# A gating kernel with larger tiles in fewer slots: 60 rows in four instead of 44 in six

## The chip, the cores and the metric

The kernel runs on one core of one Trainium2 chip. The metric is the device time of one execution in microseconds (us); the time before is the median of 9 runs.

## The reference

The input x has the shape 1x384x384x384 in bf16, the weight w1d is one number. Every channel is averaged over all 147,456 positions, the average is multiplied by the weight and put through a sigmoid, and every position of x is multiplied by the 384 numbers that result.

```python
g = jnp.einsum("bhwc->bc", x) / (H * W)
s = sigmoid(g * w1d[0])          # k = 1: one tap, no padding
return x * s[:, None, None, :]
```

So x has to be read (113.25 MB) and an output of the same size has to be written.

## The kernel before, in words

The 147,456 positions are 1152 "rows" of 128 positions: a row is a 128x384 tile in bf16, 768 bytes in each of 128 partitions. A tile of n rows is laid out so that every partition holds n x 768 bytes that are contiguous in memory on both sides (`dram`, line 172). All tiles live in one buffer, the arena.

The kernel gambles. It computes an early gate, `s_early`, from the first 4 rows alone, multiplies every tile by it and stores it, so that x is read once. Meanwhile TensorE adds up all rows, which gives the full gate, `s_true`. In the end VectorE compares the two gates bit for bit after rounding to bf16 (lines 399 to 418), and SP, ACT and VectorE read the flag `redo`. Only when it is set do they run the second pass (`again`, lines 422 to 446), which reads x again and multiplies by the full gate.

Five numbers set the tiling (line 158): the first tile has FIRST = 8 rows, the early gate is made of EARLY = 4 of them, the other 1144 rows are 26 tiles of TILE = 44 rows, which go round SLOTS = 6 places of the arena, and the first BOTH = 4 of these are loaded in two halves, one on SP's queue and one on ACT's. The first tile has its place behind the slots, at row `base` = 264.

The order of the work is written out by hand through a small planner, which keeps a stream of instructions per engine and inserts the waits that reads and writes of rows ask for:

- SP issues all other loads, in order (`load`, line 221). The load of tile k into its slot waits for the store of tile k - 6 (lines 378 to 381).
- TensorE multiplies each tile by a matrix of ones, in matmuls of 128x512 (`add_rows`, line 250), adding into three PSUM banks. It runs a loop over the slots (line 288); GpSimd waits for a tile's loads and then raises the semaphore `ready` (`relay`, line 119), on which TensorE waits at line 279.
- VectorE multiplies the tile by the early gate in place (`gate`, lines 199 to 202), after TensorE has read it, since the product overwrites the tile.
- ACT issues the store (`put`, line 316), in order, on its own DMA queue.

ACT's queue also carries the load of the weight, `w_one`, behind the first half tile (line 360); TensorE spreads the weight over the partitions (line 337) before it sums the first rows, and the early gate waits for both (line 367). After the last tile come the store of the first tile (line 387), the addition of the banks (line 390), the full gate (line 391) and the comparison. The full gate is written to the first row of the slot that the next tile would have had, `slot(26)` (line 218); the second pass first copies it to row `base` (lines 424 to 430), because its own tiles use the slots.

Of the kernel before, what the change touches and what calls it, by code (L numbers as in the profile page):

```python
# [149 lines left out]
def split(n, most):  # L150
    k = -(-n // most)
    return [n // k + (i < n % k) for i in range(k)]
# [2 lines left out]
WIDE = 512  # L155


FIRST, EARLY, TILE, SLOTS, BOTH = 8, 4, 44, 6, 4


def bass_standalone__channel_attn_eca__vision_kernel(
# [7 lines left out]
    n_rows = B * H * W // P  # L169
    x_rows, o_rows = x.flatten_outer_dims(), out.flatten_outer_dims()  # L170

    def dram(view, r0, n):
        return view[r0 * P : (r0 + n) * P, :].rearrange("(p t) c -> p (t c)", p=P)
# [10 lines left out]
    n_arena = nc.sbuf_bytes_remaining // (2 * C)  # L184
# [7 lines left out]
    def at(r0, n):  # L192
        assert r0 + n <= n_arena
        return arena[:, r0 * C : (r0 + n) * C]

    def rows(r0, n):
        return [("sb", r) for r in range(r0, r0 + n)]

    def gate(to, place, n, s):
        s_b = s[:].unsqueeze(1).broadcast_to([P, n, C])  # L200
        v, to_v = (at(r, n).rearrange("p (t c) -> p t c", t=n) for r in (place, to))
        return lambda e: e.tensor_tensor(to_v, v, s_b, ALU.mult)  # L202

    n_tiles = (n_rows - FIRST) // TILE
    base = SLOTS * TILE
    assert (n_rows - FIRST) % TILE == 0 and base + FIRST <= n_arena
    assert FIRST % 4 == EARLY % 4 == TILE % 4 == 0 and EARLY < FIRST
    last = n_tiles - 1
    ready = nc.alloc_semaphore("ready")
# [1 line left out]
    def slot(k):  # L211
        return k % SLOTS * TILE
# [2 lines left out]
        return FIRST + k * TILE  # L215


    s_true = at(slot(n_tiles), 1)
    plan = Planner(nc, "a", 70)

    def load(place, n, r0, queues=("sync",)):
# [139 lines left out]
    for k in range(BOTH, SLOTS):  # L361
# [10 lines left out]
        reads=["total", "w_scaled0", "warm1"],  # L372
        writes=["s_early"],
# [11 lines left out]
    for k in range(n_tiles - SLOTS, n_tiles):  # L385
# [8 lines left out]
            s_true, total[:], ACT_F.Sigmoid, scale=w_scaled[:, 1:2]  # L394
        ),
        reads=["total", "w_scaled1"],
        writes=["s_true"] + rows(slot(n_tiles), 1),
    )
    plan.op(
        "vector",  # L400
# [3 lines left out]
        reads=["s_true", "s_early"],  # L404
        writes=["total"],
# [4 lines left out]
        reads=["total"],  # L410
        writes=["wrong"],
# [4 lines left out]
        reads=["wrong"],  # L416
        writes=["redo"],
# [3 lines left out]

    again = Planner(nc, "b", 30)
    half, r0 = base // 2, 0
    s_kept = at(base, 1)
    again.op(
        "vector",
        lambda e: e.tensor_copy(s_kept, s_true),
        reads=rows(slot(n_tiles), 1),
        writes=["s_kept"],
    )  # L430
    for k, n in enumerate(split(n_rows, half)):
        place = k % 2 * half
        again.dma("sync", at(place, n), dram(x_rows, r0, n), writes=rows(place, n))
        again.op(
            "vector",
            gate(place, place, n, s_kept),
            reads=["s_kept"] + rows(place, n),
            writes=rows(place, n),
        )
        again.final.append(  # L440
            again.dma("scalar", dram(o_rows, r0, n), at(place, n), reads=rows(place, n))
        )
        r0 += n
# [93 lines left out]
```

## Time and profile before

| what | before |
|---|---|
| median of 9 runs | 529.23 us (528.99 to 529.73) |
| the profiled execution, its own time | 529.08 us |
| its span, first to last instruction | 527.5 us |
| TensorE busy | 246.6 us (47%) |
| VectorE busy | 241.1 us (46%) |
| DMA, bytes moved and mean rate over the span | 226.53 MB, 429 GB/s |
| one gate of 44 rows on VectorE | 8.96 us |
| store of 44 rows, median from issue to landing | 52.9 us |
| load of 44 rows, median from issue to landing | 48.0 us |
| mean granted TensorE clock | 0.740 |

How to read it: the page gives shares of busy time over the whole span, and a table by stage gives for each stretch of time its length, the busy time and number of instructions of TensorE, its weight loads, VectorE, ACT and GpSimd, then the granted TensorE clock, the mean busy share of the 16 DMA engines and the GB/s that they moved. "SPq" and "ACTq" are the DMA queues of SP and ACT, "PEq" is TensorE's sequencer. The time from issue to landing of a DMA includes its waiting behind others on its queue. Times of single packets and of landings in the text are from the trace's DMA records.

### The profile page before, as it was taken

How to read it: one execution, taken by the hardware profiler on the slowest of the kernel's cores; microseconds unless marked ns; L12 is line 12 of the kernel's file. 1: busy time of each engine (PE TensorE's matmuls, PEld its weight loads, DVE VectorE, ACT ScalarE, POOL GpSimd, SP SyncE). 2: the span in 40 equal slices, each digit the busy share in tenths (PEclk: the TensorE clock that was granted, in tenths of full speed). 3: DMA queues.
4: the chain of work that ended last, by engine and by line, in shares of the span. 5: the costliest groups of instructions: out<-in, count | busy, mean ns of one | idle time of the engine just before them, and what ended most of it. 6: DMA issues, size and time to landing. Idle time of an engine off the chain costs nothing. (4 is left out here: it accounts for less than half of the span.)

```text
span 527.5 us, 1110 instructions
## 1 busy us (share of the span) xinstructions
PE 246.6 (47%) x868; PEld 0.2 (0%) x2; DVE 241.1 (46%) x45; ACT 2.7 (1%) x4; POOL 0.3 (0%) x6
## 2 busy tenths in 40 slices
PE   0876562662551652752641642743742633734700
PEld 0000000000000000000000000000000000000000
DVE  0198626336426336236336246246156246155190
ACT  1000000000000000000000000000000000000000
POOL 0000000000000000000000000000000000000000
PEclk9997866756867867757867868757767868768765
DMA  9999999999999999999999999999999999999998
GB/s 382 432 429 410 441 425 443 418 446 425 436 438 428 443 418 446 423 438 436 430 438 423 443 425 438 436 430 438 423 443 420 441 436 428 443 420 446 416 443 358
DMA packets 8357, 226.53 MB, mean 429 GB/s; under 512 B 930, under 2 KB 930, under 8 KB 1186
## 3 DMA queue, kind: packets, MB, share of 16 engines
q10 hardware_dynamic: 4466, 121.90, 53.6%
q1 hardware_dynamic: 3888, 104.60, 46.2%
q8 instruction: 1, 0.02, 0.0%
q14 instruction: 2, 0.02, 0.0%
HBM read 113.25 MB, written 113.25 MB: 429 GB/s over the span
## 5 line engine op out<-in xcount | busy, mean ns | idle before, releaser
L238 PE MATMUL acc<-arena,ones 128*128 128x512 bf16 x863 | 245.4, 455 | 241.7 <-PEq L279 241.7
L202 DVE TENSOR_TENSOR arena<-arena,s_early 128x16896 bf16<-128x16896 bf16 (+1 forms) x27 | 234.5, 8691 | 259.5 <-PE acc L238 259.5
L337 PE MATMUL w_all<-w_one,ones 1*128 1x1 bf16 x1 | 0.2, 158 | 12.7 <-DMA w_one<-in_w1d_dram 12.7
L346 DVE TENSOR_SCALAR w_scaled<-w_all 128x1 f32<-128x1 f32 x2 | 0.2, 153 | 11.7 <-PE w_all L337 11.7
L311 DVE TENSOR_TENSOR total<-total,acc 128x128 f32<-128x128 f32 (+2 forms) x11 | 4.5, 407 | 0.3
L393 ACT ACTIVATE arena<-total,w_scaled 128x384 bf16<-128x384 f32 x1 | 0.6, 614 | 496.0 <-DVE total L311 496.0
L331 ACT ACT_TABLE_LOAD x1 | 1.3, 1283 | 2.9 <-issue 2.9
L309 DVE COPY total<-acc 128x384 f32<-128x384 f32 x1 | 0.6, 558 | 1.2 <-PE acc L238 1.2
L401 DVE TENSOR_TENSOR total<-arena,s_early 128x384 f32<-128x384 uint16 x1 | 0.6, 557 | 0.7 <-ACT arena L393 0.7
L238 PE MATMUL acc<-zeros,ones 128*128 128x512 bf16 x3 | 0.8, 379 | 0.0
L369 ACT ACTIVATE s_early<-total,w_scaled 128x384 bf16<-128x384 f32 x1 | 0.6, 616 | 12.6 <-DVE total L311 12.6
L355 DVE MEMSET ones<- 128x128 bf16 x1 | 0.2, 165 | 1.0 <-PEq L522 1.0
L236 PE MATMUL acc<-arena,ones 128*128 128x512 bf16 x1 | 0.6, 607 | 0.0
L409 DVE TENSOR_REDUCE wrong<-total 128x1 f32<-128x384 f32 x1 | 0.6, 552 | 0.0
L331 ACT ACTIVATE warm<-warm 128x1 f32<-128x1 f32 x1 | 0.2, 203 | 0.0
L415 DVE CAST redo<-wrong 128x1 int32<-128x1 f32 x1 | 0.2, 153 | 0.0
L337 PEld LDWEIGHTS w_all<-w_one,ones 1*128 1x128 bf16 x1 | 0.1, 100 | 12.7 <-issue 12.7
L236 PEld LDWEIGHTS acc<-arena,ones 128*128 128x128 bf16 x1 | 0.1, 103 | 0.0
L522 POOL MEMSET const-uint8-127<- 128x1 uint8 x1 | 0.1, 102 | 0.0
L522 POOL MEMSET const-bfloat16-1.0<- 128x1 bf16 x1 | 0.1, 101 | 0.0
L354 POOL MEMSET zeros<- 128x2 bf16 x1 | 0.1, 100 | 0.0
L353 POOL MEMSET warm<- 128x1 f32 x1 | 0.1, 99 | 0.5 <-POOLq L522 0.5
(2 smaller groups left out, 0.2 us busy)
## 6 DMA issues: line engine op xcount, KB each, us to landing
out_dram<-arena ACTq DMA_DIRECT2D x26, 4224.0 KB, 52.9
arena<-in_x_dram SPq DMA_DIRECT2D x22, 4224.0 KB, 48.0
arena<-in_x_dram ACTq DMA_DIRECT2D x4, 2112.0 KB, 26.1
arena<-in_x_dram SPq DMA_DIRECT2D x4, 2112.0 KB, 30.5
arena<-in_x_dram SPq DMA_DIRECT2D x1, 768.0 KB, 7.0
out_dram<-arena ACTq DMA_DIRECT2D x1, 768.0 KB, 16.4
w_one<-in_w1d_dram ACTq DMA_DIRECT2D x1, 0.0 KB
```

The costliest lines, as they stand in the source:

```text
L202: return lambda e: e.tensor_tensor(to_v, v, s_b, ALU.mult)
L236: loaded.append(e.matmul(bank, weights, moving, start=start, stop=stop))
L238: return e.add_instruction(mybir.InstMatmult(name=nc.get_next_instruction_name(), engine=mybir.EngineType.PE, ins=[e.lower_ap(moving), e.l ...
L309: emit = lambda e, part=part, of=of: e.tensor_copy(part, of)
L311: emit = lambda e, part=part, of=of: e.tensor_tensor(part, part, of, ALU.add)
L331: lambda e: e.activation(warm[:, 1:2], warm[:, 0:1], ACT_F.Sigmoid),
L337: lambda e: e.matmul(w_all[:, 0:1], ones[0:1, :], w_one[0:1, 0:1], start=True, stop=True),
L346: lambda e, i=i, n=n: e.tensor_scalar_mul(w_scaled[:, i : i + 1], w_all[:, 0:1], 1.0 / float(P * n)),
L369: lambda e: e.activation(s_early[:], total[:], ACT_F.Sigmoid, scale=w_scaled[:, 0:1]),
L393: lambda e: e.activation(s_true, total[:], ACT_F.Sigmoid, scale=w_scaled[:, 1:2]),
L401: lambda e: e.tensor_tensor(total[:], s_true.bitcast(U16), s_early[:].bitcast(U16), ALU.not_equal),
L409: lambda e: e.reduce_max(wrong[:], total[:], axis=mybir.AxisListType.X),
```

## The change

The five numbers become FIRST = 12, EARLY = 4, TILE = 60, SLOTS = 4 and BOTH = 3. The first tile has 12 rows, of which the early gate still uses 4; the other 1140 rows are 19 tiles of 60 rows, which go round four places; the first three are loaded in halves of 30 rows on both queues, the fourth whole on SP's. In the arena 252 rows hold tiles, where it was 272. The full gate gets a row of its own behind the first tile, so its activation no longer counts as a write to a slot, and the second pass uses it there without a copy.

```diff
-FIRST, EARLY, TILE, SLOTS, BOTH = 8, 4, 44, 6, 4
+FIRST, EARLY, TILE, SLOTS, BOTH = 12, 4, 60, 4, 3
...
-    assert (n_rows - FIRST) % TILE == 0 and base + FIRST <= n_arena
+    assert (n_rows - FIRST) % TILE == 0 and base + FIRST < n_arena
...
-    s_true = at(slot(n_tiles), 1)
+    s_true = at(base + FIRST, 1)
...
-        writes=["s_true"] + rows(slot(n_tiles), 1),
+        writes=["s_true"],
...
-    s_kept = at(base, 1)
-    again.op(
-        "vector",
-        lambda e: e.tensor_copy(s_kept, s_true),
-        reads=rows(slot(n_tiles), 1),
-        writes=["s_kept"],
-    )
...
-            gate(place, place, n, s_kept),
-            reads=["s_kept"] + rows(place, n),
+            gate(place, place, n, s_true),
+            reads=rows(place, n),
```

## The prediction

> **What bounds the kernel now.** I read the page first: the engine shares, the 40 slices, the DMA totals.
>
> ```profile
> DMA  9999999999999999999999999999999999999998
> GB/s 382 432 429 410 441 425 443 418 446 425 436 438 428 443 418 446 423 438 436 430 438 423 443 425 438 436 430 438 423 443 420 441 436 428 443 420 446 416 443 358
> DMA packets 8357, 226.53 MB, mean 429 GB/s; under 512 B 930, under 2 KB 930, under 8 KB 1186
> HBM read 113.25 MB, written 113.25 MB: 429 GB/s over the span
> ```
>
> The DMA engines are busy in every slice, while TensorE and VectorE are under half busy. The bytes are those of reading x once and writing the output once, and no tile size changes them. So I cut the span at the landing of the first store (62.66), of store 20 (461.94), of the last load (490.36) and at the issue of the last large store (509.36), and asked for a table by stage.
>
> ```profile
> 0.00:62.66 62.66, 37.77 (x139) 0.20 (x2) 31.95 (x13) 2.10 (x3) 0.33 (x6) 0.92 1.00 417
> 62.66:461.94 399.28, 188.74 (x660) 0.00 (x0) 178.99 (x21) 0.00 (x0) 0.00 (x0) 0.72 1.00 433
> 461.94:490.36 28.42, 9.60 (x33) 0.00 (x0) 15.83 (x2) 0.00 (x0) 0.00 (x0) 0.73 1.01 436
> 490.36:509.36 19.00, 10.47 (x36) 0.00 (x0) 8.99 (x2) 0.00 (x0) 0.00 (x0) 0.77 0.99 428
> 509.36:527.50 18.14, 0.00 (x0) 0.00 (x0) 5.33 (x10) 0.61 (x1) 0.00 (x0) 0.50 0.89 380
> ```
>
> The last column is GB/s. The middle is flat at 433; only the head (417) and the last 18 us (380) are below. At 433.4 the 226.53 MB take 522.7 us, so 4.8 of the 527.5 us are all that is not plain transfer: 1.05 us to the first packet, about 1.1 us more in the head (10-us windows there show 369 and 409 GB/s), and the rest in the last microseconds, where the 16 engines end between 525.4 and 527.1.
>
> Then the waits of the queues and the groups, for whether something else is near to ending late:
>
> ```profile
> SPq L109 <- DMA out_dram<-arena: 431.2, 20, 58.4
> SPq L474 <- DVE redo L415: 73.3, 1, 73.3
> ```
>
> ```profile
> L238 PE MATMUL acc<-arena,ones 128*128 128x512 bf16 x863 | 245.4, 455 | 241.7 <-PEq L279 241.7
> L202 DVE TENSOR_TENSOR arena<-arena,s_early 128x16896 bf16<-128x16896 bf16 (+1 forms) x27 | 234.5, 8691 | 259.5 <-PE acc L238 259.5
> ```
>
> SP's load waits each time for the store of its slot, and TensorE and VectorE wait for tiles: the slots pace everything, the DMA engines set the rate. Last, the timeline of the end:
>
> ```profile
> 490.51 9.82 PE L238 MATMUL acc<-arena,ones 128*128 128x512 bf16 x33 [10.45 <-PEq L279]
> 500.37 10.63 DVE L202 TENSOR_TENSOR arena<-arena,s_early 128x16896 bf16<-128x16896 bf16 x2 [11.30 <-PE acc L238]
> 510.91 2.68 DVE L311 TENSOR_TENSOR total<-total,acc 128x384 f32<-128x384 f32 x6
> 515.46 0.15 DVE L415 CAST redo<-wrong 128x1 int32<-128x1 f32 x1
> ```
>
> The last tile goes load, sum, gate, store, and during its sum and gate the DMA engines live on the stores that are still waiting. That is the place the change touches.
>
> **What the Trainium skill says.** "DMA: Bandwidth & Descriptors", section Where 436 GB/s comes from, gives a fabric ceiling of 435.2 GB/s; the trace agrees, with 433 to 436 in full windows, for loads alone, stores alone and both. Its section Queues, rings and completion order says that each DMA engine goes round robin between the queues that have work; the trace agrees: with both queues full, a load and a store of 44 rows take 19.96 us together, and stores alone 9.97 us each. Its section Latency and other measured facts gives about 600 ns from an HWDGE issue to its first byte; the trace shows more, 1.05 us on SP's first load and 2.34 us on ACT's. "TensorE: Matmul & The Clock Gate", Part 1, says that the array starts at half clock and is released after about 3.4 us of work; the trace agrees: matmul starts of a tile are 427 ns apart for 6 to 12 of them, then 216 ns.
>
> **The change, part by part.** Names: tile k, its load and store k. A row (128x384 bf16) costs 9.97/44 = 0.2266 us of all DMA engines alone. T is when a store lands, 0.4 us after its last packet (527.09 and 527.47 at the end).
>
> Bytes and DMA work: none added. A DMA engine handles 464 data packets before (8 for each of 26 stores, 22 loads, 8 halves and the first tile both ways); after, 19 stores, 16 loads, 6 halves and the two small ones make 43 x 8 = 344. A packet's fixed cost is bounded by its recorded time (1251 ns for 33,792 B, 629 for 16,896: 7 ns fixed) and by the spacing of rows in the last stores (1.81 us for 8 rows, 9.97 for 44: none). So 120 packets save 0 to 0.84 us; I take 0.4, half way. Without a stall the last landing moves from 527.47 to 527.1.
>
> Head: the first tile is 12 rows, and w_one follows a half tile of 30 rows on ACT's queue instead of 22, so s_early comes some 4 to 6 us later. Cover: loads need 252 rows x 0.2266 = 57.1 us of transfers anyway. Tile 0, landed at 17.1 before, waits for 20 rows more of its own order and some 8 of its rival's: 23.4. Its sum is 9.22 + 12 x 0.216 = 11.8, its gate 8.96 x 60/44 = 12.2, so store 0 is issued near 47.4 (35.6 before), with some 52 rows of loads still queued. If the cover were gone, each us of delay would cost one. Nothing here; the irregular 1.1 us of the head may move by half a microsecond either way. The first three loads on both queues instead of four: the same DMA engines, nothing.
>
> Middle: two transfers of 60 rows take 120 x 0.2269 = 27.2 us. From a load's landing until its store can start: 0.15 to TensorE (490.36 to 490.51), sum 45 matmuls, gate 12.2, two hand-overs of 0.03, and the store's first packet. The sum is the 8.8 to 9.8 us of 33 matmuls plus 12 warm ones of 0.216: 11.4 to 12.4, I take 11.9. First packet after issue: never seen on a busy chip; 1.05 to 2.34, I take 1.4, nearer to the cleaner record. Sum 0.15 + 11.9 + 12.2 + 0.06 + 1.4 = 25.7. The DMA engines ask for that store two stores later (54.4 us after the landing of the store three back), so 25 us are spare in the middle. What does change is the load queue: store 0 lands about as the last early load ends, so SP's queue runs dry for 0.4 + 1.4 = 1.8 us per round, while the stores take the full rate: no loss. It leaves the loads ending d after the store three back landed: with w = 1.8 of stores alone, the next load still has w to do alone-equivalent when that store ends, shared, so d = 2w = 3.6 (1.8 if the queue just doesn't run dry, up to one 1.7-us packet more, since a packet isn't interrupted).
>
> End: this is the only path. Before: store 21 landed 481.94, the last load 8.4 later; stores 22 to 24 end 3 x 9.97 + 4.2 - 0.4 = 33.7 after it, at 515.6 (the trace has 515.69 as landing); store 25, issued 509.36, could start at 510.8: 4.8 us spare. After: call T the landing of store 15. Stores 16 and 17 end at T + 2 x 13.6 + 1.8 - 0.4 = T + 28.6. Load 18 lands at T + 3.6, its store can start at T + 3.6 + 25.7 = T + 29.3. **The spare 4.8 us become a stall of 0.7 us.** Then 72 rows, whatever they wait for. The span becomes 527.5 - 0.4 + 0.7 = 527.8.
>
> The row for s_true: s_true no longer waits for store 20's slot. ACT ran it at 513.63, directly after the sum, so that wait cost nothing; the removed copy is in the second pass, which isn't run (the records show no line of it). The checks end some 5 us after the base gate, about T + 36 (T + 3.6 + 24.3 + 2.4 + 5), before the last landing near T + 46: hidden by 72 rows of stores; no cost.
>
> Sum: 527.8 against 527.5, so 529.08 + 0.3 = 529.4 for the profiled execution, which lies 0.15 below the median of 529.23; on the median, 529.5.
>
> **The rivals.** (1) *A longer stall at the end: slower.* With a first packet after 2.34 us, w is 2.74, d 5.5: the store can start at T + 5.5 + 26.6 = T + 32.1, the others end at T + 27.2 + 2.7 - 0.4 = T + 29.5; stall 2.6, and 3.1 with a cold sum of 12.4: 529.23 - 0.4 + 2.6 = 531.4. For it: ACT's own first issue took 2.34. Against: that one ran beside SP's first issue. It decides from a stall of 1.5 us on (first packet at about 1.8). (2) *Faster.* No stall (d = 1.8, first packet at 1.05), the whole 0.84 us of packets, and the 0.55 us that the 40-to-50 window loses (409 against 433) where small loads meet large stores: 529.23 - 1.39 = 527.8. For it: fewer, larger packets. Against: the steady rate is at the ceiling, and the spacing shows next to no fixed cost. (3) *Four slots don't cover the loop*, and the store queue runs dry in the middle: it needs the 25.7 us to exceed 54.4 - 3.6, twice what is read; each microsecond beyond would cost some 15 us, so 544 for one. Nothing in the profile speaks for it. (4) That the change doesn't act: the built order shows loads and stores of 128x23040 and halves of 11520 elements, so it does; it would give 529.2.
>
> **How the numbers follow.** A measurement here can tell about 0.2%, 1.06 us. The main case, the tail meeting within 1 us (528.2 to 530.3), 52%; rival 1, 30%; rival 2, 15%; rival 3, 3%. Likeliest 529.5. The range, 528.2 to 531.6, runs from no stall with all packet savings and a little of the head to rival 1 with its price; it leaves out the far end of rival 2 and rival 3, and the worst sum of bounds. Faster 0.15, same 0.52, slower 0.33.
>
> **What would show it.** GB/s of 433 in the middle as before; SP's queue waiting for stores in each round; load 18 landing near 485; the last sum near 11.9 and gate near 12.2; the last large store issued near 509 to 511, and in the windows just after it a dip in DMA share of 0.5 to 1 us. Wrong if DMA share dips in the middle, if the head's loss changes by over 0.6 us, or if the store before the last lands well after the last one is issued plus 1.4.

## The result, and the profile after

The changed kernel takes 533.07 us (median of 10 runs, 531.39 to 537.94) against 529.21; the ratio is put at 1.0082, with a 95% interval of 1.0065 to 1.0099 (the two medians alone give 1.0073). It is slower by some 0.8%, and it varies: the runs of before lie within 0.7 us, these within 6.5. Two executions in the experiments below (541.98 and 538.65 us) fell in a slower state, over 1.5% above the fastest run of their kernel, and are left out of medians and ranges. Nine more runs of the same kernel, in two sets beside the experiments, gave 531.84 and 531.42; over all 19 the median is 531.84, 2.6 us above before. The profiled execution is one of the quick ones: 531.1 us, span 529.5, that is 2.0 more than the span of before, where the prediction had 0.3.

The slices of the page look as before, but for the last but one (348 GB/s, where it was 443), and the rate over the span is 428 GB/s, where it was 429.

```profile
DMA  9999999999999999999999999999999999999988
GB/s 388 425 440 409 432 446 421 421 439 446 446 411 425 446 442 442 418 425 446 442 432 418 435 442 439 418 428 442 442 442 418 425 446 439 442 414 432 436 348 368
DMA packets 6196, 226.52 MB, mean 428 GB/s; under 512 B 690, under 2 KB 690, under 8 KB 690
```

The table by stage, cut at the landing of store 0 (74.48), of store 15 (480.60), of the last load (487.44) and at the issue of the last large store (511.00), has the place in its fourth line. The columns are those of before; the last two are DMA share and GB/s.

```profile
0.00:74.48 74.48, 41.34 (x160) 0.20 (x2) 39.21 (x12) 2.10 (x3) 0.33 (x6) 0.86 1.00 422
74.48:480.60 406.12, 174.44 (x662) 0.00 (x0) 177.57 (x15) 0.00 (x0) 0.00 (x0) 0.72 1.00 434
480.60:487.44 6.84, 0.00 (x0) 0.00 (x0) 4.80 (x1) 0.00 (x0) 0.00 (x0) 0.50 1.00 431
487.44:511.00 23.56, 11.82 (x48) 0.00 (x0) 12.19 (x2) 0.00 (x0) 0.00 (x0) 0.79 0.89 382
511.00:529.50 18.50, 0.00 (x0) 0.00 (x0) 6.13 (x10) 0.61 (x1) 0.00 (x0) 0.50 0.90 383
```

Head and middle are as good as they were (434 GB/s in the middle). Between the last load and the issue of its store the DMA share falls to 0.89, where the same stage of before had 0.99: 11% of 23.56 us is 2.6 us of idle DMA engines. Windows of 2 us put it in place; first the kernel after, then the kernel before.

```profile
506.00:508.00 2.00, 0.00 (x0) 0.00 (x0) 2.00 (x1) 0.00 (x0) 0.00 (x0) 0.50 0.85 369
508.00:510.00 2.00, 0.00 (x0) 0.00 (x0) 2.00 (x1) 0.00 (x0) 0.00 (x0) 0.50 0.22 92
510.00:512.00 2.00, 0.00 (x0) 0.00 (x0) 2.00 (x2) 0.00 (x0) 0.00 (x0) 0.50 0.87 369
```

```profile
508.00:510.00 2.00, 0.00 (x0) 0.00 (x0) 2.00 (x2) 0.00 (x0) 0.00 (x0) 0.50 0.94 406
510.00:512.00 2.00, 0.00 (x0) 0.00 (x0) 1.93 (x4) 0.00 (x0) 0.00 (x0) 0.50 0.94 406
```

(A packet of 46,080 bytes takes 1.7 us, so windows of 2 us swing a little with where it is counted; a fall to 92 GB/s is no swing.) VectorE is busy all the while, with the gate of the last tile: the stores before it are done, and the DMA engines wait for the gate. The timeline gives the chain: the last load landed at 487.44, then

```profile
487.60 11.17 PE L238 MATMUL acc<-arena,ones 128*128 128x512 bf16 x45 [14.39 <-PEq L279]
498.61 0.81 PE L238 MATMUL acc<-zeros,ones 128*128 128x512 bf16 x3
498.81 12.16 DVE L202 TENSOR_TENSOR arena<-arena,s_early 128x23040 bf16<-128x23040 bf16 x1 [13.41 <-PE acc L238]
```

and the store's issue at 511.00, its first packet at 511.84.

The DMA records allow one more view. On one DMA engine the next packet starts 3 to 4 ns before the recorded end of the last, so the 16 sequences can be told apart, and a gap or a long packet found in each (where two engines end within a few ns of each other, their sequences can be swapped, so the figures that follow hold to about 0.2 us). After: all 16 engines stand idle before 511.9, the latest for about 1.0 us, the other 15 for 1.7 to 3.3. Before: no engine has such a gap. And after, the latest engine is late for a reason of its own: six of its load packets in the middle took 65 to 790 ns longer than the usual 1702, 1.68 us in all. Eight more slow load packets, 1.45 us together, are spread over other engines. Before, no packet between 100 and 490 us was more than 27 ns over.

### The profile page after: what moved, and what is told of

It reads as the page before. It is cut to its first block, busy times and chain, and to the rows that moved or that the text cites. A ratio compares the mean times of both kernels' runs of the same rounds, so it can differ in the third digit from the quotient of the medians.

```text
span 529.5 us, 1069 instructions
## 1 busy us (share of the span) xinstructions
PE 227.6 (43%) x868; PEld 0.2 (0%) x2; DVE 239.9 (45%) x38; ACT 2.7 (1%) x4; POOL 0.3 (0%) x6
## 5 line engine op out<-in xcount | busy, mean ns | idle before, releaser
L202 DVE TENSOR_TENSOR arena<-arena,s_early 128x23040 bf16<-128x23040 bf16 (+1 forms) x20 | 233.3, 11677 | 260.3 <-PE acc L238 260.3
L238 PE MATMUL acc<-arena,ones 128*128 128x512 bf16 x863 | 226.5, 430 | 256.2 <-PEq L279 256.2
L236 PE MATMUL acc<-arena,ones 128*128 128x512 bf16 x1 | 0.6, 607 | 0.0
```

The lines of the kernel that those rows point to most:

```text
L236: loaded.append(e.matmul(bank, weights, moving, start=start, stop=stop))
L238: return e.add_instruction(mybir.InstMatmult(name=nc.get_next_instruction_name(), engine=mybir.EngineType.PE, ins=[e.lower_ap(moving), e.l ...
```

## Experiments

Two theories. **TAIL**: the chain of the last tile (landing, sum, gate, store) has lost its cover, so that all DMA engines wait for it. **MIDDLE**: with four slots, or with packets of 46,080 bytes, single DMA engines lose time all along, and the end adds little. The kernels differ from the changed one only by the edits named; of each the main lines are shown. "Late" below is the time by which a load lands after the store that landed just before it, and the stall is counted on the latest and on the earliest DMA engine.

**The changed kernel again** (twice, for other executions).

> The changed kernel as it is, once more, for a second execution's trace and the spread. Theory TAIL (the last tile's landing, sum, gate and store have lost their cover, so every DMA engine waits for them at the end): median near 533, and in the trace a gap of 1 to 3 us or more in the DMA engines' work just before the last large store, the middle at 433 GB/s as before. Theory MIDDLE (with four slots the load queue runs dry in each round, and with 46,080-byte packets single DMA engines lose time there): the excess is already there when store 15 lands, as a lag of the slowest DMA engine behind the others of 3 us or more, and the end adds about 1 us.

> The changed kernel as it is, beside the three others of this set on the same chip. 531 to 534, a stall of all DMA engines before the last large store of 3 us or more (1 to 2 on the latest of them).

Measured: 531.84 (530.68 to 532.71) and 531.42 (530.99 to 532.25). Windows of the first one's trace:

```profile
508.00:510.00 2.00, 0.00 (x0) 0.00 (x0) 2.00 (x1) 0.00 (x0) 0.00 (x0) 0.50 0.16 69
510.00:512.00 2.00, 0.00 (x0) 0.00 (x0) 2.00 (x1) 0.00 (x0) 0.00 (x0) 0.50 0.05 23
512.00:514.00 2.00, 0.00 (x0) 0.00 (x0) 2.00 (x2) 0.00 (x0) 0.00 (x0) 0.50 0.87 369
```

Here 15 engines are idle for 3.1 to 5.0 us and the latest for about 1.4. Both theories have a share: one engine again collected slow load packets (nine, 2.9 us in all), it landed the last load 3.5 us after the first engine, and since the sum waits for all 16, the other 15 paid for it at the end.

**The last tile in halves.** `put` gates and stores in as many parts as it is told:

```diff
-        put(slot(k), TILE, row0(k))
+        put(slot(k), TILE, row0(k), 2 if k == last else 1)
```

> The changed kernel, but the last tile is gated and stored in two halves of 30 rows, so that its first store can start 6.1 us earlier; the middle is untouched. TAIL: the stall of 1.1 us (slowest DMA engine) to 3.2 us (the others) is gone, the span is near 527.6 and the median 529.0 to 529.5, with executions within about 1 us as for the kernel before. MIDDLE: only the 1 to 2 us of the end go, median 531 to 532, and the spread of several us stays.

Measured: 529.51 (20 runs, 528.72 to 532.59), ratio to before 1.0011 (1.0001 to 1.0021). In the trace (532.25 us, one of the longest executions) the first half's store is issued at 509.38; the latest engine has no gap, most others 1.0 to 1.6 us, because that one engine is about 5 us late: ten or eleven of its load packets were slow, 4.3 to 4.8 us in all, one of them by 1.4.

```profile
508.00:510.00 2.00, 0.00 (x0) 0.00 (x0) 2.00 (x2) 0.00 (x0) 0.00 (x0) 0.50 0.16 69
510.00:512.00 2.00, 0.00 (x0) 0.00 (x0) 2.00 (x1) 0.00 (x0) 0.00 (x0) 0.50 1.06 449
514.00:527.00 13.00, 0.00 (x0) 0.00 (x0) 7.58 (x11) 0.61 (x1) 0.00 (x0) 0.50 0.95 404
527.00:530.60 3.60, 0.00 (x0) 0.00 (x0) 0.00 (x0) 0.00 (x0) 0.00 (x0) 0.50 0.05 23
```

The last line is that engine alone, at a sixteenth of the rate. So an edit of the last tile alone takes back 2.3 of the 2.6 us: TAIL holds for the median. A spread of 3.9 us stays, and in this trace it is as MIDDLE has it: the time went in the middle, on one engine.

**Slots and tile size apart.** Five slots of 52 rows; four slots of 44 rows, plain and with the last tile in halves (with four slots three tiles, not four, are loaded in halves, as in the changed kernel).

```diff
-FIRST, EARLY, TILE, SLOTS, BOTH = 12, 4, 60, 4, 3
+FIRST, EARLY, TILE, SLOTS, BOTH = 8, 4, 52, 5, 4
...
+FIRST, EARLY, TILE, SLOTS, BOTH = 8, 4, 44, 4, 3
```

> First tile 8 rows, 22 tiles of 52 rows in five slots, first four on both queues; else as the changed kernel. After the last load lands, three stores of 11.8 us are still to go instead of two of 13.6, against a chain of about 22 us. TAIL: some 8 us of cover, no stall, 529.0 to 529.5 and a small spread. MIDDLE, if packets of more than 33,792 bytes are to blame: half of the excess, 530.5 to 532; if the dry load queue is: 531 to 533.

> The old tile of 44 rows (first tile 8) in four slots, first three on both queues: fewer slots alone. TAIL: after the last load lands two stores of 10.0 us cover a chain of about 19.5 us plus half of the load's lateness of 4 to 7 us, a stall of 2 to 3.5 us: 531 to 533. MIDDLE, if the dry load queue is to blame: 532 to 534 with a large spread; if the larger packets are: 529.2 to 530.5.

> 44-row tiles in four slots with the last tile gated and stored in halves (22 rows each, so the first store starts 4.5 us earlier, against a stall of 3.8 us on the slowest DMA engine). TAIL: the stall is gone or under 1 us, 529.2 to 530.5 instead of 534.8. MIDDLE, by the number of slots: stays above 532. MIDDLE, by the size of packets: as TAIL, and with the small spread of the kernel before, since packets have 33,792 bytes.

Measured: 52 in five 529.45 (528.76 to 530.62), ratio 1.0007 (0.9998 to 1.0015), so neither slower nor faster than before; 44 in four 534.81 (533.13 to 535.71), ratio 1.0098 (1.0074 to 1.0122); with halves 529.49 (18 runs, 528.71 to 532.81). Five slots have no gap at the end (first line); four slots of the old tile have a hole of about 4.4 us on the latest engine and 6.1 on the earliest (the other three):

```profile
508.00:510.00 2.00, 0.00 (x0) 0.00 (x0) 1.93 (x4) 0.00 (x0) 0.00 (x0) 0.50 0.83 359
```

```profile
512.00:514.00 2.00, 0.00 (x0) 0.00 (x0) 2.00 (x1) 0.00 (x0) 0.00 (x0) 1.00 0.75 321
514.00:516.00 2.00, 0.00 (x0) 0.00 (x0) 2.00 (x1) 0.00 (x0) 0.00 (x0) 0.56 0.00 0
516.00:518.00 2.00, 0.00 (x0) 0.00 (x0) 2.00 (x1) 0.00 (x0) 0.00 (x0) 0.50 0.00 0
```

So it is the number of slots that costs: 44 rows take 534.81 in four slots and 529.20 in six (the run of the next part). The larger tile with the four slots makes it less bad, not worse: two stores of 60 rows cover more than two of 44. My expectation of 531 to 533 was too low because the loads were 9.2 us late there, not 4 to 7. By slots the spread is 0.7 (six, 12 runs), 1.9 (five, 12 runs), 3.9 and 4.1 (four, with the last tile in halves; tiles of 60 rows, 20 runs, and of 44, 18 runs).

The equal spread of the last two doesn't mean an equal cause. With 44 rows in four slots no load packet between 100 and 490 us is more than 40 ns over the usual 1251, in either trace, although the one with halves is of a long execution (531.44 us). Its time goes at the end: on one engine the last load ends 2.4 us after the next, 15 engines wait 2.0 to 3.3 us for the first half's store and the latest 0.4.

```profile
514.00:516.00 2.00, 0.00 (x0) 0.00 (x0) 2.00 (x2) 0.00 (x0) 0.00 (x0) 1.00 0.04 17
```

In the seven traces with 60 rows in four slots, whole loads, and all sums and gates, 6 to 23 load packets are that slow. So the spread of times comes with four slots in both, but slow load packets were seen only with the larger tile, and packet size stays a candidate for them.

**The parts that should do nothing.** The row of its own for the full gate, with the five numbers of before; and on top of it the last tile in halves.

> The changed source with the five numbers of before (8, 4, 44, 6, 4): the row of its own for the full gate, alone. Both theories: nothing, 529.0 to 529.5. If the wait for the slot was worth something, below 529.0.

> As the run before it, with the last tile gated and stored in two halves. TAIL: the cover at the end is there already (4.8 us), so nothing: 529.0 to 529.5. If storing in halves helps by itself: below 528.8.

Measured: 529.20 (ratio 1.0001, 0.9992 to 1.0010) and 529.28 (1.0003, 0.9994 to 1.0012). Both nothing: the row is free, and halves help only where the cover is missing.

**Loads in two parts.** Meant to tell packet size from distance in memory. The last tile is in halves as above, and the fourth early load is split likewise:

```diff
-            load(slot(k), TILE, row0(k))
+            load(slot(k), TILE, row0(k), ("sync", "sync"))
```

> As the run with the last of 60 rows in halves, but every whole load is issued as two loads of 30 rows on the same queue (packets of 23,040 bytes, at the same distance of 46,080 bytes in memory); stores keep 46,080. If the size of load packets makes one DMA engine lag (5.1 us at the end in the run with halves alone): no lag beyond 2 us and executions within 1 us, median 528.7 to 529.2. If it is the distance in memory or the four slots: lag and spread as there, 528.7 to 532.6.

Measured: 554.80 (553.88 to 555.98). It doesn't decide what it was meant for, since it changed something larger. The records show the DMA engines alternating between the queues packet by packet, so loads of 23,040-byte packets beside stores of 46,080 get a third of the bytes (between 60 and 70 us 1.45 MB of loads, 2.86 MB of stores). The stores race ahead, and at the end there are none left to cover the last loads and their sums:

```profile
500.00:530.00 30.00, 13.56 (x52) 0.00 (x0) 13.77 (x2) 0.00 (x0) 0.00 (x0) 0.72 0.63 269
530.00:536.00 6.00, 0.00 (x0) 0.00 (x0) 6.00 (x2) 0.00 (x0) 0.00 (x0) 0.87 0.14 61
```

Not all of the loss is there: from 60 to 500 us the rate is 423 GB/s, where the changed kernel had 434 in its middle, and nearly 200 packets of each queue took over 25 ns longer than is usual for their size.

**How late the loads land.** Two edits meant to bring store 0 to land before the fourth load: all early loads on SP's queue, and the first tile gated and stored in halves (alone, and with the last tile in halves too).

```diff
-        load(slot(k), TILE, row0(k), ("sync", "scalar"))
+        load(slot(k), TILE, row0(k))
...
-            put(slot(k), TILE, row0(k - SLOTS))
+            put(slot(k), TILE, row0(k - SLOTS), 2 if k == SLOTS else 1)
```

> The changed kernel, with the first three tiles loaded whole on SP's queue, so that store 0 starts earlier and lands before the fourth load does: the load queue doesn't run dry, and each load then lands about 4.4 us after the store three back instead of 6.8. TAIL: half of that difference goes from the stall, 1.0 to 1.5 us less than the changed kernel beside it, so 529.8 to 532. If the lateness of the loads has no part in the stall: as the changed kernel.

> The changed kernel, with the first tile (not the last) gated and stored in two halves, so that store 0 starts 6 us earlier and lands before the fourth load does. If the load queue's running dry at that moment (first packet 4 us after the issue) is what makes every later load land 6.8 us after the store three back: the lateness falls to 3 to 5 us, the stall at the end by half of the difference, and the median to 530 to 531 from 531.8. If the lateness has another source: it stays at 6.8, and so does the median.

> The first and the last tile both gated and stored in halves. TAIL: no stall, and more cover than with the last tile alone, so that a DMA engine that lags delays the last store less: 528.6 to 529.4, with a spread below the 4 us of the last tile alone. If the lag itself is what is left: 528.7 to 532 as there.

Measured: one queue 532.94 (five runs, 532.04 to 538.17, ratio 1.0072, 1.0052 to 1.0093); first tile in halves 533.06 (531.64 to 533.97); first and last 530.23 (19 runs, 528.90 to 533.96). The first two expectations failed, because neither edit did what it should; the third run fell on its second branch, and wider. Store 0 was issued earlier (43.25, 43.34 and 41.67 instead of 48.93) but landed at 77.69, 74.26 and 74.43 instead of 74.48. Its first packet came 4.1 to 4.7 us after its issue, on an empty queue beside a full one; and the halves, being smaller packets, got less than half of the rate, as above; the lateness stayed at 6.8 to 7.7. With one queue the fourth load and store 0 ended together, the loads became 10.4 us late, and the stall grew to 3.1 us on the latest engine and 8.7 on the earliest: the lateness sets the stall, in the direction not intended. In the last of the three, one engine had fourteen slow packets, nearly all of them loads, and ended 4 us after the rest: more cover doesn't remove the lag. The trace with the first tile in halves has its slow packets on most engines at once, within 4 us near 115 us, and none later.

**Without the sums, without the gates.**

```diff
-            add_rows(e, 1, slot(s) * C, TILE, False, False).then_inc(
+            add_rows(e, 1, slot(s) * C, 4, False, False).then_inc(
...
-            gate(place, place, n, s_early),
+            gate(place, place, 1, s_early),
```

> The changed kernel, with only 3 of the 45 matmuls per tile (the full sum is left out, and the comparison is of the early gate with itself), so that the last store can start about 10 us earlier and TensorE hardly reads the arena. TAIL: no stall; 528.5 to 529.2. If TensorE's reading makes the single DMA engine late that lags in the middle: executions within 1 us and a lag under 1 us; if not: a spread of several us as in the run with halves, 528.5 to 532.5.

> The changed kernel, with the gate on one of the 60 rows of each tile (the other rows are stored as they were read), so that the last store can start about 12 us earlier and VectorE hardly touches the arena. TAIL: no stall; 528.5 to 529.2. If VectorE's traffic makes the single DMA engine lag: executions within 1 us; if not: a spread of several us, 528.5 to 532.5.

> A second trace of the kernel with 3 of 45 matmuls per tile (the full sum is left out, and the comparison is of the early gate with itself), whose executions fell in two groups, near 528.0 and near 530.0, with one traced in the first group. If a single DMA engine's lag makes the second group: one engine ends 2 us after the others. If the stall at the end does: all wait before the last large store.

Measured: few sums 530.05 (20 runs, 527.90 to 535.58: three near 528.0, fifteen from 529.6 to 530.5, two above 533), and 527.85 in one more execution; few gates 529.85 (20 runs, 529.23 to 531.62). The stall is gone in all three traces, as TAIL has it; here around the last large store of the first, issued at 505.84:

```profile
504.00:506.00 2.00, 0.00 (x0) 0.00 (x0) 2.00 (x2) 0.00 (x0) 0.00 (x0) 0.50 1.22 530
506.00:508.00 2.00, 0.00 (x0) 0.00 (x0) 2.00 (x1) 0.00 (x0) 0.00 (x0) 0.50 0.85 369
```

But both medians lie above the 528.5 to 529.2 that TAIL expected, and executions still spread (with few gates 19 of 20 within 1 us). In the traces slow load packets are nearly gone: none and one of 49 ns with few sums, one of 409 ns with few gates. Both traced executions with few sums fell in the quick group, though, and that with few gates was among its quickest, so this doesn't show that TensorE's or VectorE's traffic makes packets slow, nor that it doesn't. Which engine, or what else, makes the group near 530 wasn't seen. It stays open.

## Why the prediction was wrong, point by point

The direction, the place and the mechanism were among its cases (rival 1: a stall of the DMA engines before the last large store), but the likeliest case had that stall at 0.7 us and no change, and the range ended at 531.6. Rival 1's own price, 531.4, lies near the 531.84 of all runs, but partly by luck: it took 2.34 us for the first packet of loads and stores alike (measured 4.1 and 0.84) and had 2.6 us of stall on the latest engine, where the three traces of the changed kernel show 1.0 to 1.5, and it had no lag. In its own steps:

1. *What bounds it*: right. 434 GB/s in the middle after, 433 before. (The section of the Trainium skill that the prediction cites for the ceiling, "DMA: Bandwidth & Descriptors", Where 436 GB/s comes from, also says that about 358 GB/s binds transfers between HBM and SBUF; the measurement decides, and it is above that.)
2. *Packets*, 0.4 us saved: nothing speaks against it. The twelve engines that don't lag would have ended between 525.1 and 525.7 without the gap (528.4 less 2.6 to 3.3), against 525.5 to 526.4 for most before: about 0.3 to 0.5.
3. *Head*: right. Store 0 issued at 48.93 (47.4 worked out), with no loss of DMA time.
4. *Middle, 25 us to spare*: right. The store queue didn't run dry (store 16 was issued 22.4 us before store 15 landed).
5. *The chain from the last landing to the first packet of the store*, 25.7: too long, measured 23.56 + 0.84 = 24.4. The sum took 11.17 (11.9 taken), the first packet 0.84 on idle engines (1.4 taken). The two other traces of this kernel have 23.9 and 24.0 to the issue. (The prediction's check on before, 515.6 against 515.69, sets an end of packets against a landing; the packets ended at 515.25, so with its own 1.4 the spare time was 4.5 us, not 4.8.)
6. **A step that failed: "d = 2w = 3.6", how late the loads land.** Measured 6.84, 7.14 and 6.82. SP's queue ran dry once, not in each round: from the landing of the last early load at 69.02, 5.5 us before store 0, until load 4's first packet. And d rests on the 1.4 us taken for that first packet. On idle engines that is too much, but at the place where it was used it is far too little: load 4, issued at 74.50 on an empty queue beside a full one, had its first packet at 78.61, 4.1 us later. In that time store 1 went ahead by three packets, and the loads stayed four packets of 1.70 us late for the rest of the run. With the measured numbers the prediction's own formula fits: from T = 480.60, stores 16 and 17 end at T + 27.2 + 3.4 - 0.4 = 510.8 (measured 510.9), and the store can start at T + 6.84 + 24.4 = 511.84 (measured 511.84). Stall 1.0 us, as on the latest engine in the records. The rule d = 2w isn't confirmed by this: w = 0.4 + 4.1 would give 9.0, and 6.84 is measured. Against the 0.7 of the prediction the too small d adds 1.6 (half of 3.2), and the too long chain of step 5 takes 1.3 back. That 0.7 came so near is luck, and the two errors together account for 0.3 of the 1.7 us by which the span was missed (529.5 for 527.8).
7. **The larger part, a term put at nothing: one DMA engine that lags (in the profiled execution).** The sum "527.5 - 0.4 + 0.7" takes it that every DMA engine gets through the middle as it did before. After, in four of the traces with 60-row tiles, one engine loses 1.1 to 2.9 us in slow load packets, and in the two with the last tile in halves over 4; since the last tile's sum waits for all 16, this lag delays the last store of all, with no cover to absorb it. In the profiled execution the engines reach the end of store 17 between 508.7 and 510.9. Without slow packets on any engine the last load would have landed near 485.7 and the store started near 510.1, 1.7 us earlier (an estimate: the engines that don't lag had their part of the last load by 483.7, and the landing came 2.05 us after the latest part); without those of the latest engine alone, 0.9 earlier, for the next one lags too. How much of the spread of the runs comes from this isn't shown: the long execution of 44 rows in four slots had a late engine and no slow packets.
8. *The row of its own*, nothing: right, by its own run.

From 511.85 on, 72 rows take 16.3 us, so most engines end at 528.3 to 528.4; one ends at 528.99, beside an instruction fetch of 0.31 us at 525.8, and the landing follows 0.45 later: the span of 529.5. Before, two fetches of this size (at 521.2) fell on engines that were early and cost nothing; one of 16 KB, at 495.2, hit the engine that ended last, at 527.09, 0.2 us after the next. After a stall all engines start level, so here the fetch came at its full price.

What stays open: why load packets of one engine get slow in the 60-row kernel with four slots, and, in the traces, not with six slots of 44, five of 52 or four of 44. Packet size, slots, how short before its start a load is issued, and the traffic of TensorE and VectorE were not told apart. The lag was traced, not switched off: no run shows what the changed kernel would take without it.

## What to carry to other kernels

Where DMA engines set the rate, look at the last tile: from its landing to its store's first packet other transfers have to be queued for the whole chain, and fewer slots take away just these. What counts is the time of the stores still waiting, less the chain; something has to be left of it, as a reserve for the latest of the 16 engines. Before, 5 us were left; here it was 1 short. Splitting the last tile's gate and store bought it back in both kernels with four slots, and did nothing with six.

## What the runs showed of the hardware

- A DMA issued on an empty queue while the other queue is full had its first packet 3.8 to 4.9 us after the issue (load 4: 3.9 to 4.7 with packets of 46,080 bytes, 3.9 and 4.1 with 33,792; store 0: 3.8 to 4.9), and 0.84 us on idle engines. The Trainium skill ("DMA: Bandwidth & Descriptors", Latency and other measured facts) has about 600 ns from an HWDGE issue; the measurement decides. The prediction had taken 1.4 us for both cases.
- The turn between queues goes by packets, here one partition's run of a tile whatever its length, so the bytes divide as the packet sizes do (1.45 MB to 2.86 between 60 and 70 us). Splitting the loads alone cost 25.3 us (554.80 against 529.51).
- Bytes per DMA engine and time are the same for packets of 33,792 and of 46,080: 9.97 us for 44 rows, 13.6 for 60.
- A fetch of 16 KB of instructions takes one DMA engine about 1.3 us (a gap of 0.9 and a packet longer by 0.4), in the middle of a stream (before, at 495.2; after, at 495.1).
